# A linear-attention stage with w turned by row halves and its decay scans handed on between half-chunks

## The chip, the cores and the metric

The kernel runs on one core of a Trainium2 chip. Its engines work from queues of their own and meet at semaphores: PE (TensorE), VectorE (DVE in the profile), ScalarE (ACT), GpSimd (POOL), and SP, which here only issues DMAs. Times are device microseconds of one execution; the time before is the median of three runs.

## The reference

Three stages follow each other: a linear attention with decay (B = 4, H = 8, S = 768 tokens, D = 48), a mixture of eight experts of which each token takes the best one, and a dense layer with a squared relu. Only the first stage is touched by the change:

```python
for t in range(S):
    kt, vt, rt, wt = (k[:, :, t], v[:, :, t], r[:, :, t], w[:, :, t])
    cur = np.einsum('bhd,bhe->bhde', u[None] * kt, vt)
    y[:, :, t] = np.einsum('bhd,bhde->bhe', rt, state + cur)
    state = wt[:, :, :, None] * state + np.einsum('bhd,bhe->bhde', kt, vt)
```

## The kernel before, in words

The attention runs over 16 units (`NU`); a unit is one batch row and two heads (`pr`), so that 2 x 64 partitions hold two heads, each padded from 48 to 64. A unit's 768 tokens are `NC` = 6 chunks of `C` = 128. Inputs come in as `nat` tiles with tokens on the partitions.

For one unit the stages are these. `w_turn` (L670) transposes w on PE into two PSUM banks `z`, three chunks in each; a chunk takes `L` = 129 columns, with a zero column between chunks that was set once. `suffix` (L680) scans one bank backwards on VectorE: products of w from a position to the end of its chunk, `suf`. `prefix` (L690) takes the reciprocal of each chunk's whole product as the start (three columns of `f_1`) and scans the same bank forwards, `ff`. Each works on one bank, so a unit has four scans. `k_turn` and `r_turn` (L699, L704) transpose k and r, each into two banks by row halves (twelve 64-row transposes), and VectorE multiplies them with `suf` and `ff` into kT and rA. `scores` (L728) multiplies kT and rA on PE; ScalarE copies the result and GpSimd masks it (L737). `k_back` turns kT back into kP, `states` (L740) multiplies kP with v; for chunk 0 it multiplies with `none`, 64 zero columns of `f_1`. `state_scan` (L747) scans the result on VectorE. `bonus_in`, `within` and `across` add three parts of y in PSUM, `back` transposes y to rows. `gate_products` (L709) are two GpSimd multiplications of 128 x 576 into g1, a tile with one buffer; `gate_sum` (L715) sums it on VectorE, `gate_values` (L719) multiplies v with the sum on GpSimd for bonus_in.

The order on every engine is the order in which the code is written (manual_schedule). The loop `for t in range(-1, NU + 1)` (L838) is a period: it works on unit t and prepares units t + 1 and t + 2. The second half of suffix and prefix of unit t + 1 stands at the head of a period, the first half for unit t + 2 near its end, behind `gate_sum` and `gate_values` of unit t + 1. `step` inserts, by the tables PLAN and LAST, pieces of `route_steps` (L160): the choice of experts for a finished batch row, with many small VectorE operations and scatters by GpSimd. It falls on periods t = 4 to 9, 8 to 13 and 12 to 15.

PSUM banks of the transposes, scores and states come from a ring of four in turn (`Ring`, L642). Within a period the order is scores (2), k_back (2), states (1), scores (2), k_turn (2), r_turn (2), back (2), so the second bank of k_turn is the one that states used.

A load into a `nat` tile is issued by SP at the head of a period, for the unit two periods on (v: one, w: three).

Of the kernel before, what the change touches and what calls it, by code (L numbers as in the profile page):

```python
# [9 lines left out]
F32 = mybir.dt.float32  # L10
# [4 lines left out]
ALU = mybir.AluOpType  # L15
# [6 lines left out]
def rwkv_moe_kernel(  # L22
# [15 lines left out]
    nc = tc.nc  # L38
    B, H, S, D = r.shape
    NT, DM = out.shape  # L40
    E, _, F = w1.shape
    F2 = w_in.shape[1]
    C = 128
    NC = S // C
    HC = NC // 2
    L = C + 1
    HP = H // 2
    KD = DM // 128
    KF = F // 128
# [22 lines left out]
    ident = cst.tile([128, 128], F32, name="ident")  # L72
# [249 lines left out]
    def load_expert(pool, w1e, w2e, hf, into=None):  # L322
        t, t2 = into or (pool.tile([128, KD, F // 2], F32, name="w1r"), pool.tile([128, KF // 2, DM], F32, name="w2r"))
        nc.sync.dma_start(t, w1e.rearrange("o (c p) f -> p (o c) f", p=128)[:, :, hf * (F // 2):(hf + 1) * (F // 2)])
        nc.sync.dma_start(t2, w2e.rearrange("o (c p) d -> p (o c) d", p=128)[:, hf * (KF // 2):(hf + 1) * (KF // 2)])
        return t, t2
# [228 lines left out]
    def first_block(P):  # L555
        return Block(P, NA, w1[0:1], w2[0:1], lambda n, i: gA[:n, 0, i:i + 1])
# [16 lines left out]
    def route_step():  # L573
        return next(routing[B - 1], 0)

    with ExitStack() as actx:
        actx.enter_context(tc.manual_schedule(engines={ET.PE, ET.DVE, ET.Activation, ET.SP, ET.Pool}))
        ac = actx.enter_context(tc.tile_pool(name="ac", bufs=1))
        wk = actx.enter_context(tc.tile_pool(name="wk", bufs=2))
        ps_a = actx.enter_context(tc.tile_pool(name="ps_a", bufs=1, space=PSUM))  # L580
        ps_u = actx.enter_context(tc.tile_pool(name="ps_u", bufs=2, space=PSUM))
        ps_y = actx.enter_context(tc.tile_pool(name="ps_y", bufs=2, space=PSUM))

        NU = B * HP
        HL = HC * L
        NBUF = {"w": 2, "k": 2, "r": 2, "v": 3}
        PAD = {"w": 1.0, "k": 0.0, "r": 0.0, "v": 0.0}
        nat = {(nm, i): ac.tile([128, NC, 2, 64], F32, name=f"{nm}N{i}") for nm in "wkrv" for i in range(NBUF[nm])}
        u_bc = ac.tile([128, H, D], F32, name="u_bc")
        f_1 = ac.tile([128, 1 + NC * L], F32, name="f1")  # L590
        s_1 = ac.tile([128, 1 + HL], F32, name="s1")
        bonus = [ac.tile([128, NC, 2, 64], F32, name=f"gv{i}") for i in range(2)]
        start = [ac.tile([128, 64, NC], F32, name=f"St{i}") for i in range(2)]
        prod = [ac.tile([128, D, NC], F32, name=f"P{i}") for i in range(3)]
        bia = cst.tile([128, 16], F32, name="bia")
        warm = bia[0:1, 2:3]
        none = f_1[:, 2:66]
        zw = [ps_u.tile([128, 1 + HL], F32, name="zw") for _ in range(2)]
        first_z = [ps_y.tile([128, 1 + HL], F32, name="py") for _ in range(2)]
        xTs, xrs = {}, {}  # L600

        def pad(nm, i, eng):
# [9 lines left out]
        def setup_first():  # L612
# [11 lines left out]
            for z in (*zw, *first_z):  # L624
                nc.vector.memset(z[:, ::L], 0.0)
            nc.vector.memset(s_1, 0.0)
            nc.vector.memset(s_1[:, ::L], 1.0)
            nc.vector.memset(f_1, 0.0)
# [23 lines left out]
        class Unit:  # L652
# [15 lines left out]
                return pt  # L668

            def w_turn(self, z=zw):  # L670
                for c in range(NC):
                    hf, ci = divmod(c, HC)
                    nc.tensor.transpose(z[hf][:, 1 + ci * L:1 + ci * L + C], self.wN[:, c].rearrange("p h d -> p (h d)"), ident)

            def w_check(self):
                sq = wk.tile([128, 2 * NC, D], F32, name="sq", bufs=1)
                nc.scalar.activation(sq, self.wN[:, :, :, :D].rearrange("p c h d -> p (c h) d"), AF.Square, bias=bia[:, 0:1])
                nc.scalar.activation(sq, sq, AF.Relu, bias=bia[:, 1:2], accum_out=viol[:, self.un:self.un + 1])

            def suffix(self, hf, z=zw):  # L680
                if hf == 0:
                    self.suf = wk.tile([128, 1 + NC * L], F32, name="suf")
                    self.ff = wk.tile([128, 1 + NC * L], F32, name="ff")
                    self.sufv = self.suf[:, 1:].rearrange("p (c x) -> p c x", x=L)
                    self.fv = self.ff[:, 0:NC * L].rearrange("p (c x) -> p c x", x=L)
                at = hf * HL
                nc.vector.tensor_tensor_scan(out=self.suf[:, at:at + HL + 1][:, ::-1], data0=z[hf][:, ::-1], data1=s_1[:, ::-1],
                                             initial=0.0, op0=ALU.mult, op1=ALU.add)

            def prefix(self, hf, z=zw):  # L690
                at, cs = hf * HL, slice(hf * HC, hf * HC + HC)
                nc.vector.reciprocal(f_1[:, 0:NC * L].rearrange("p (c x) -> p c x", x=L)[:, cs, 0:1], self.sufv[:, cs, 0:1])
                nc.vector.tensor_tensor_scan(out=self.ff[:, at:at + HL], data0=z[hf][:, :HL], data1=f_1[:, at:at + HL],
                                             initial=0.0, op0=ALU.mult, op1=ALU.add)

            def spread(self):
                nc.scalar.copy(self.P[:, :, 1:], self.sufv[:, 1:, 0:1].rearrange("p c o -> p o c").to_broadcast([128, D, NC - 1]))

            def k_turn(self):  # L699
                self.kT = wk.tile([128, NC, C], F32, name="kT")  # L700
                for q, pt in enumerate(self.turn(self.kN.rearrange("p c h d -> p c (h d)"))):
                    nc.vector.tensor_tensor(self.kT[:, :, 64 * q:64 * q + 64], pt, self.sufv[:, :, 1 + 64 * q:65 + 64 * q], op=ALU.mult)

            def r_turn(self):  # L704
                self.rA = wk.tile([128, NC, C], F32, name="rA", bufs=3)
                for q, pt in enumerate(self.turn(self.rN.rearrange("p c h d -> p c (h d)"))):
                    nc.vector.tensor_tensor(self.rA[:, :, 64 * q:64 * q + 64], pt, self.fv[:, :, 64 * q:64 * q + 64], op=ALU.mult)  # L707

            def gate_products(self):  # L709
                eng = nc.vector if self.un == NU - 1 else nc.gpsimd  # L710
# [74 lines left out]
        def at(i, st, *a):  # L785
            if 0 <= i < NU:
                getattr(units[i], st)(*a)
# [21 lines left out]
        def first_block_step(t, place):  # L809

            if t == NU - 3 and place == "loads":
                blkA = first["A"] = first_block(P)
                blkA.upto = NT - S + 1
                words = [load_expert(raw, w1[0:1], w2[0:1], hf) for hf in range(2)]
                blkA.w1r, blkA.w2r = ({hf: words[hf][q] for hf in range(2)} for q in range(2))
            if NU - 2 <= t < NU and place == "back":
                for f in range(2 * (t - NU + 2), 2 * (t - NU + 2) + 2):
                    first["A"].prep_w(f, nc.vector, part="hi")
            if (t, place) == (NU - 1, "back"):
                rows_A(rw)  # L820
            if t == NU - 1 and place == "turned":
                for f in range(FA):
                    first["A"].prep_w(f, nc.vector, part="lo")
            if t == NU - 1 and place == "gate":
                first["A"].gather()
            if t == NU and place == "back":
                first["A"].scale(nc.vector)
            if t == NU and place == "turned":
                routing[B - 1] = route_steps(B - 1, xTs[B - 1], xrs[B - 1], rw, ps_t)
                route_step()  # L830

        setup_first()
        at(0, "w_turn", first_z)
        at(0, "suffix", 0, first_z)
        at(0, "prefix", 0, first_z)
        at(0, "w_check")
        routing_constants()
        for t in range(-1, NU + 1):  # L838
            z = first_z if t == -1 else zw
            load("w", w, t + 3)  # L840
            if t >= 0:
                load("v", v, t + 1)
                load("k", k, t + 2)
                load("r", r, t + 2)
            first_block_step(t, "loads")
            at(t, "scores", 0)
            at(t, "k_back")
            at(t + 2, "w_check")
            step(t, "back")
            first_block_step(t, "back")  # L850
            if t + 1 < NU - 1:
                at(t + 1, "gate_products")
            at(t + 1, "suffix", 1, z)
            at(t + 1, "prefix", 1, z)
            if t == 0:
                at(t, "gate_sum")
                at(t, "gate_values")
            at(t - 1, "within")
            at(t, "states")
            at(t, "state_scan")  # L860
            at(t, "scores", 1)
            at(t + 1, "spread")
            at(t - 1, "across")
            step(t, "scan")
            at(t + 1, "k_turn")
            at(t + 1, "r_turn")
            step(t, "turned")
            first_block_step(t, "turned")
            at(t + 2, "w_turn")
            at(t, "bonus_in")  # L870
            if t + 1 == NU - 1:
                at(t + 1, "gate_products")
            if t >= 0:
                at(t + 1, "gate_sum")
                at(t + 1, "gate_values")
            at(t + 2, "suffix", 0)
            at(t + 2, "prefix", 0)
            step(t, "gate")
            first_block_step(t, "gate")
            if t < NU:  # L880
                at(t - 1, "back")
            step(t, "end")
# [64 lines left out]
    with tc.If(rare > 0, label="rare"):  # L947
        fine = nc.values_load(flag[0:1, 0:1], min_val=0, max_val=1)
        with tc.If(fine == 0):
# [42 lines left out]
            with ExitStack() as fctx:  # L992
# [6 lines left out]
                for b in range(B):  # L999
                    nc.sync.dma_start(xr[:, :, :DM], x_tok[b * S:(b + 1) * S].rearrange("(c p) m -> p c m", p=C))  # L1000
                    for c in range(NC):
                        nc.vector.tensor_copy(xp[:, :, :D], xr[:, c, :DM].rearrange("p (h d) -> p h d", d=D))
                        pt = ps_x.tile([128, 512], F32, name="px")
# [389 lines left out]
```

## Time and profile before

| | |
|---|---|
| median of 3 runs | 838.42 us (837.02 to 838.67) |
| profiled execution | 837.48 us, span 835.6 us |
| PE busy | 805.9 us, 96% |
| VectorE busy | 534.2 us, 64% |
| ScalarE busy | 374.3 us, 45% |
| GpSimd busy | 352.3 us, 42% |
| granted TensorE clock, mean | 0.986 |

The page gives busy time for each engine over the whole span, slices of the span, the chain that ended last and the costliest groups. A timeline lists instructions by start and length (consecutive ones of a kind merged, with their count); in brackets stands how long the engine was idle before and what released it. [...]

### The profile page before, as it was taken

Reading aid. Unit: us, or ns where it says so; the run is one execution under the profiler, and the core shown is the slowest. Engines: PE = TensorE matmul, PEld = TensorE weight load, DVE = VectorE, ACT = ScalarE, POOL = GpSimd, SP = SyncE. Lnnn points to the kernel's source line nnn. Section 1 sums busy time; section 2 is a strip of 40 time slices with the busy share of each in tenths; the row PEclk is TensorE's granted clock in tenths of the full one; section 3 lists DMA queues with packets and bytes.
Section 4 is the critical chain, followed back from the end, with each engine's and each line's share of the span. In section 5 each row is a group of like instructions: output and inputs, shape, how many; then the busy total and the mean of one; then the engine's idle time right before and its main releaser. Section 6 shows DMA issues by size and latency. Waiting matters only on the chain.

```text
span 835.6 us, 15492 instructions
## 1 busy us (share of the span) xinstructions
PE 805.9 (96%) x5868; PEld 731.1 (87%) x5868; DVE 534.2 (64%) x961; ACT 374.3 (45%) x792; POOL 352.3 (42%) x433
## 2 busy tenths in 40 slices
PE   6999999979999999999999999999999999999995
PEld 5988887869889999999999998888899999999994
DVE  7889898946666777887534788888533434434342
ACT  4666665532555455455554343434333333333321
POOL 8666868624434545644752333333211212213121
PEclk9999999969999999999999999999999999999998
DMA  9775769215758676768651232231204213022011
GB/s 181 151 137 115 163 141 271 94 26 179 263 91 214 172 208 219 221 168 248 181 174 33 75 132 76 94 111 62 75 1 142 77 38 114 19 95 76 1 48 38
DMA packets 157365, 102.89 MB, mean 123 GB/s; under 512 B 112351, under 2 KB 140943, under 8 KB 157287
## 3 DMA queue, kind: packets, MB, share of 16 engines
q1 hardware_dynamic: 149046, 86.55, 38.7%
q0 software_dynamic: 4912, 14.65, 5.2%
q8 instruction: 47, 0.77, 0.4%
q10 hardware_dynamic: 3328, 0.66, 0.4%
q14 instruction: 32, 0.25, 0.1%
HBM read 79.34 MB, written 22.50 MB: 122 GB/s over the span
## 4 chain that ended last, share of the span: by engine, by line
PE 59%; issue 12%; POOL 4%; DVE 0%; POOLq 0%; ACT 0%; DVEq 0%; ACTq 0%
PE ph L345 10%; PE ph L344 10%; PE ph L346 10%; PE po L344 5%; PE po L346 5%; PE po L345 5%; PE px L346 5%; PE px L344 5%; PE px L345 5%; POOL out_dram L1182 2%; PE px L430 1%; PE po L430 0%; POOL x22l L339 0%; POOL x21l L339 0%; POOL x20l L339 0%
## 5 line engine op out<-in xcount | busy, mean ns | idle before, releaser
L1157 DVE SCALAR_TENSOR_TENSOR gg<-ph,rl 128x512 f32<-128x512 f32 x96 | 66.2, 690 | 121.6 <-ACT rl L1155 121.6
L1155 ACT ACTIVATE rl<-ph 128x512 f32<-128x512 f32 x96 | 57.4, 598 | 146.4 <-PE ph L346 146.3
L339 DVE TENSOR_TENSOR gl<-gg,gh 128x512 fp32r<-128x512 f32 x96 | 67.0, 697 | 65.9 <-ACT gh L337 41.9
L337 ACT CAST gh<-gg 128x512 fp32r<-128x512 f32 x96 | 59.6, 621 | 103.6 <-DVE gg L1157 103.6
L339 POOL TENSOR_TENSOR w1l<-w1r,w1h 128x384 fp32r<-128x384 f32 x56 | 59.4, 1067 | 66.7 <-ACT w1h L337 66.3
L333 ACT ACTIVATE hh<-ph 128x320 fp32r<-128x320 f32 (+7 forms) x64 | 32.4, 507 | 113.4 <-PE ph L346 107.0
L1103 POOL TENSOR_TENSOR caf<-caf,cbf 128x384 f32<-128x384 f32 x32 | 32.5, 1016 | 114.0 <-DVE cbf L1102 114.0
L339 DVE TENSOR_TENSOR w2l<-w2r,w2h 128x384 fp32r<-128x384 f32 x64 | 64.3, 1007 | 20.1 <-ACT w2h L337 19.5
L334 DVE SCALAR_TENSOR_TENSOR hl<-ph,hh 128x320 fp32r<-128x320 f32 (+7 forms) x64 | 36.9, 576 | 38.3 <-ACT hh L333 38.0
L1182 POOL DMA_INDIRECT out_dram<-ob,tokc x24 | 23.4, 974 | 67.2 <-DVE ob L1180 65.0
L344 PE MATMUL po<-hh,w2h 128*128 128x320 f32 (+4 forms) x120 | 42.8, 357 | 0.0
L345 PE MATMUL po<-hl,w2h 128*128 128x320 f32 (+4 forms) x120 | 41.6, 347 | 0.0
L346 PE MATMUL po<-hh,w2l 128*128 128x320 f32 (+4 forms) x120 | 41.6, 347 | 0.0
L339 POOL TENSOR_TENSOR x22l<-x2r,x22h 128x512 fp32r<-128x512 f32 x12 | 15.5, 1296 | 51.5 <-ACT x22h L337 51.5
L339 POOL TENSOR_TENSOR x21l<-x2r,x21h 128x512 fp32r<-128x512 f32 x12 | 15.5, 1293 | 45.5 <-ACT x21h L337 45.5
L734 PE MATMUL pt<-rA,kT 64*128 64x128 f32 x300 | 31.7, 302 | 2.7 <-DVE rA L707 2.7
L400 POOL DMA_INDIRECT xg<-x_rows,gi x28 | 29.0, 1036 | 11.4 <-issue 5.1
L337 ACT CAST w2h<-w2r 128x384 fp32r<-128x384 f32 x64 | 33.0, 517 | 0.0
L737 POOL TENSOR_SCALAR_AFFINE_SELECT A<-A 128x768 f32<-128x768 f32 x32 | 28.1, 878 | 11.0 <-ACT A L736 10.0
L337 ACT CAST w1h<-w1r 128x384 fp32r<-128x384 f32 x64 | 32.7, 512 | 0.0
L245 POOL DMA_INDIRECT x_rows<-xr,dsi x24 | 24.1, 1003 | 20.3 <-DVE dsi L232 15.3
L339 POOL TENSOR_TENSOR x20l<-x2r,x20h 128x512 fp32r<-128x512 f32 x12 | 15.5, 1291 | 35.9 <-ACT x20h L337 35.9
(859 smaller groups left out, 2661.8 us busy)
## 6 DMA issues: line engine op xcount, KB each, us to landing
w1r<-in_moe_w_dram SPq DMA_DIRECT2D x16, 768.0 KB, 5.5
w2r<-in_moe_w_dram SPq DMA_DIRECT2D x16, 768.0 KB, 7.5
x2r<-x_cols SPq DMA_DIRECT2D x12, 768.0 KB, 4.8
cq<-in_moe_w_in_dram SPq DMA_DIRECT2D x16, 384.0 KB, 5.8
cq<-in_moe_w_out_dram SPq DMA_DIRECT2D x16, 384.0 KB, 8.0
vN<-in_v_dram SPq DMA_DIRECT2D x32, 144.0 KB, 3.9
part<-ob SPq DMA_DIRECT2D x24, 192.0 KB, 2.0
ob<-part SPq DMA_DIRECT2D x24, 192.0 KB, 2.6
```

The source lines that it names most:

```text
L333: nc.scalar.activation(hi, src, AF.Relu)
L334: nc.vector.scalar_tensor_tensor(lo, src, 0.0, hi.bitcast(F32), op0=ALU.max, op1=ALU.subtract)
L337: nc.scalar.copy(hi, src)
L339: lo_eng.tensor_tensor(lo, src, hi.bitcast(F32), op=ALU.subtract)
L344: nc.tensor.matmul(out_, a_of(ah), b_of(bh), start=start, stop=False)
L345: nc.tensor.matmul(out_, a_of(ah), b_of(bl), start=False, stop=False)
L346: nc.tensor.matmul(out_, a_of(al), b_of(bh), start=False, stop=stop)
L734: nc.tensor.matmul(pa[j][:, ci], self.kT[pp, hf * HC + ci], self.rA[pp, hf * HC + ci], start=True, stop=True)
L1103: nc.gpsimd.tensor_tensor(af, af, bf, op=ALU.add)
L1155: nc.scalar.activation(rl, ph, AF.Relu)
L1157: nc.vector.scalar_tensor_tensor(gg, ph, 0.0, rl, op0=ALU.max, op1=ALU.mult)
L1182: ins = nc.gpsimd.indirect_dma_start(out=out[:, :], out_offset=IndirectOffsetOnAxis(ap=tokc[:, n:n + 1], axis=0), in_=ob, in_offset=None)
```

## The change

Each chunk of 128 tokens is cut into two halves of 64 (`HT`). Bank q of `z` now holds half q of all six chunks, 65 columns each (`NL` = 390), and w_turn uses twelve 64-row transposes. The suffix products of the first halves need the product of the second halves: suffix scans bank 1, a copy of six columns puts the products into `f_1`, and bank 0 is scanned with them as starts. In prefix it is the other way round: reciprocal, scan of bank 0, copy of six columns into `f_1`, scan of bank 1. Both scans of suffix for unit t + 2 now stand near the end of the period, both of prefix for unit t + 1 at the head. `suf` and `ff` get an axis for the half, and spread, k_turn and r_turn read them so. gate_products of unit t + 1 moves from behind the first routing pieces to ahead of scores, to the head of the period.

```diff
-    L = C + 1
+    HT = C // 2
+    L = HT + 1
+    NL = NC * L
...
-        f_1 = ac.tile([128, 1 + NC * L], F32, name="f1")
-        s_1 = ac.tile([128, 1 + HL], F32, name="s1")
+        f_1 = ac.tile([128, NL + 1], F32, name="f1")
+        s_1 = ac.tile([128, NL + 1], F32, name="s1")
...
-        none = f_1[:, 2:66]
+        none = f_1[:, 1:L]
...
             def w_turn(self, z=zw):
+
                 for c in range(NC):
-                    hf, ci = divmod(c, HC)
-                    nc.tensor.transpose(z[hf][:, 1 + ci * L:1 + ci * L + C], self.wN[:, c].rearrange("p h d -> p (h d)"), ident)
+                    for q in range(2):
+                        p = slice(HT * q, HT * q + HT)
+                        nc.tensor.transpose(z[q][:, c * L + 1:c * L + L], self.wN[p, c].rearrange("p h d -> p (h d)"), ident[p, p])
...
-                at = hf * HL
-                nc.vector.tensor_tensor_scan(out=self.suf[:, at:at + HL + 1][:, ::-1], data0=z[hf][:, ::-1], data1=s_1[:, ::-1],
-                                             initial=0.0, op0=ALU.mult, op1=ALU.add)
-
-            def prefix(self, hf, z=zw):
-                at, cs = hf * HL, slice(hf * HC, hf * HC + HC)
-                nc.vector.reciprocal(f_1[:, 0:NC * L].rearrange("p (c x) -> p c x", x=L)[:, cs, 0:1], self.sufv[:, cs, 0:1])
-                nc.vector.tensor_tensor_scan(out=self.ff[:, at:at + HL], data0=z[hf][:, :HL], data1=f_1[:, at:at + HL],
-                                             initial=0.0, op0=ALU.mult, op1=ALU.add)
+            def suffix(self, z=zw):
+
+                self.suf = wk.tile([128, 2, NL + 1], F32, name="suf")
+                for q in (1, 0):
+                    if q == 0:
+                        nc.vector.tensor_copy(f_1[:, L::L], self.suf[:, 1, 1::L])
+                    nc.vector.tensor_tensor_scan(out=self.suf[:, q, ::-1], data0=z[q][:, ::-1], data1=(s_1 if q else f_1)[:, ::-1],
+                                                 initial=0.0, op0=ALU.mult, op1=ALU.add)
+
+            def prefix(self, z=zw):
+
+                self.ff = wk.tile([128, 2, NL], F32, name="ff")
+                for q in range(2):
+                    if q == 0:
+                        nc.vector.reciprocal(f_1[:, 0:NL:L], self.suf[:, 0, 1::L])
+                    else:
+                        nc.vector.tensor_copy(f_1[:, 0:NL:L], self.ff[:, 0, HT::L])
+                    nc.vector.tensor_tensor_scan(out=self.ff[:, q], data0=z[q][:, :NL], data1=f_1[:, :NL], initial=0.0, op0=ALU.mult, op1=ALU.add)
...
-        at(0, "suffix", 0, first_z)
-        at(0, "prefix", 0, first_z)
+        at(0, "suffix", first_z)
...
             first_block_step(t, "loads")
+            if t + 1 < NU - 1:
+                at(t + 1, "gate_products")
             at(t, "scores", 0)
...
-            if t + 1 < NU - 1:
-                at(t + 1, "gate_products")
-            at(t + 1, "suffix", 1, z)
-            at(t + 1, "prefix", 1, z)
+            at(t + 1, "prefix", z)
...
-            at(t + 2, "suffix", 0)
-            at(t + 2, "prefix", 0)
+            at(t + 2, "suffix")
```

## Rows read from the trace of the kernel before

**Rows 1.** Busy time by stretch: microseconds and instructions of each engine, granted clock, DMA.

```profile
15.00:165.00 150.00, 143.82 (x2388) 127.45 (x2384) 133.96 (x268) 94.67 (x230) 103.79 (x132) 0.99 0.68 153
```

**Rows 2.** Waits to 180 us: microseconds in total, times, longest.

```profile
DVE kT L702 <- PE pt L667: 6.3, 6, 1.4
```

**Rows 3.** Timeline of VectorE, period t = 3: start, length, operation, idle before.

```profile
37.88 0.74 DVE L717 TENSOR_REDUCE g<-g 128x12 f32<-128x576 f32 x1
38.54 0.96 DVE L687 TENSOR_TENSOR_SCAN suf<-zw,s 128x388 f32<-128x388 f32 x1
39.53 0.18 DVE L692 RECIPROCAL f<-suf 128x3 f32<-128x3 f32 x1
39.74 0.96 DVE L693 TENSOR_TENSOR_SCAN ff<-zw,f 128x387 f32<-128x387 f32 x1
40.62 0.94 DVE L687 TENSOR_TENSOR_SCAN suf<-zw,s 128x388 f32<-128x388 f32 x1
...
42.69 0.73 DVE L749 TENSOR_TENSOR_SCAN St<-pt,P 128x288 f32<-128x288 f32 x1
44.60 0.56 DVE L702 TENSOR_TENSOR kT<-pt,suf 128x384 f32<-128x384 f32 x1 [1.18 <-PE pt L667]
...
46.47 0.74 DVE L717 TENSOR_REDUCE g<-g 128x12 f32<-128x576 f32 x1
```

**Rows 4.** Timeline of GpSimd, the same period.

```profile
38.76 1.15 POOL L720 TENSOR_TENSOR gv<-vN,g 128x576 f32<-128x576 f32 x1 [2.69 <-PE pt L667]
...
40.92 1.42 POOL L712 TENSOR_TENSOR g<-kN,rN 128x576 f32<-128x576 f32 x1
42.42 1.41 POOL L713 TENSOR_TENSOR g<-g,u_bc 128x576 f32<-128x576 f32 x1
```

**Rows 5.** Timeline of PE, the same period and the end of the one before.

```profile
35.82 0.54 PE L667 MATMUL pt<-ident,rN 64*128 64x64 f32 x12
36.29 0.87 PE L673 MATMUL zw<-ident,wN 128*128 128x128 f32 x6
37.00 0.82 PE L758 MATMUL py<-ident,gv 128*128 128x128 f32 x6
...
38.17 0.89 PE L734 MATMUL pt<-rA,kT 64*128 64x128 f32 x12
...
41.78 0.37 PE L734 MATMUL pt<-rA,kT 64*128 64x128 f32 x1
...
43.98 0.59 PE L667 MATMUL pt<-ident,kN 64*128 64x64 f32 x12
```

**Rows 6.** Groups by shape (busy, mean ns), two timeline rows, and one line's shortest, median, longest.

```profile
L258 DVE COPY vA<-vals 128x3 f32<-128x3 f32 x1 | 1.2, 1152 | 0.0
...
L237 DVE COPY vals<-cum 128x8 f32<-128x8 f32 x2 | 0.3, 165 | 0.0
...
101.09 1.46 DVE L190 SCALAR_TENSOR_TENSOR cand<-z,e 128x48 f32<-128x48 f32 x1
...
101.06 1.43 POOL L713 TENSOR_TENSOR g<-g,u_bc 128x576 f32<-128x576 f32 x1
...
L692 DVE RECIPROCAL f<-suf x32: 178/178/181, 6.1 to 151.1; 128x3 f32<-128x3 f32 x32
```

**Rows 7.** Timeline of PE's weight loads, period t = 12: k_turn's second bank.

```profile
130.60 0.14 PEld L667 LDWEIGHTS pt<-ident,kN 64*128 64x128 f32 x1 [0.19 <-DVE St L749]
```

**Rows 8.** Timeline of GpSimd and of PE, period t = 0.

```profile
16.04 1.40 POOL L712 TENSOR_TENSOR g<-kN,rN 128x576 f32<-128x576 f32 x1 [1.33 <-DVE g L717]
...
18.89 1.15 POOL L720 TENSOR_TENSOR gv<-vN,g 128x576 f32<-128x576 f32 x1
...
20.48 0.82 PE L758 MATMUL py<-ident,gv 128*128 128x128 f32 x6
```

**Rows 9.** Timeline of PE and of VectorE, period t = 9.

```profile
101.69 0.27 PE L667 MATMUL pa<-ident,kN 64*128 64x64 f32 x1
...
104.02 0.53 DVE L702 TENSOR_TENSOR kT<-pa,suf 128x384 f32<-128x384 f32 x1
```

More of the change, by code (lines that the diff above doesn't have):

```diff
@@ L584, in rwkv_moe_kernel @@
         NU = B * HP
-        HL = HC * L
         NBUF = {"w": 2, "k": 2, "r": 2, "v": 3}
@@ L596, in rwkv_moe_kernel @@
         warm = bia[0:1, 2:3]
-        none = f_1[:, 2:66]
-        zw = [ps_u.tile([128, 1 + HL], F32, name="zw") for _ in range(2)]
-        first_z = [ps_y.tile([128, 1 + HL], F32, name="py") for _ in range(2)]
+        none = f_1[:, 1:L]
+        zw = [ps_u.tile([128, NL + 1], F32, name="zw") for _ in range(2)]
+        first_z = [ps_y.tile([128, NL + 1], F32, name="py") for _ in range(2)]
         xTs, xrs = {}, {}
@@ L678, in w_check @@
                 nc.scalar.activation(sq, sq, AF.Relu, bias=bia[:, 1:2], accum_out=viol[:, self.un:self.un + 1])
[L680 to L685, printed above, removed]
-                at = hf * HL
-                nc.vector.tensor_tensor_scan(out=self.suf[:, at:at + HL + 1][:, ::-1], data0=z[hf][:, ::-1], data1=s_1[:, ::-1],
-                                             initial=0.0, op0=ALU.mult, op1=ALU.add)
@@ L696, in spread @@
             def spread(self):
-                nc.scalar.copy(self.P[:, :, 1:], self.sufv[:, 1:, 0:1].rearrange("p c o -> p o c").to_broadcast([128, D, NC - 1]))
+                nc.scalar.copy(self.P[:, :, 1:], self.suf[:, 0, L + 1::L].rearrange("p (o c) -> p o c", o=1).to_broadcast([128, D, NC - 1]))
             def k_turn(self):
@@ L701, in k_turn @@
                 for q, pt in enumerate(self.turn(self.kN.rearrange("p c h d -> p c (h d)"))):
-                    nc.vector.tensor_tensor(self.kT[:, :, 64 * q:64 * q + 64], pt, self.sufv[:, :, 1 + 64 * q:65 + 64 * q], op=ALU.mult)
+                    nc.vector.tensor_tensor(self.kT[:, :, 64 * q:64 * q + 64], pt, self.suf[:, q, 1:].rearrange("p (c x) -> p c x", x=L)[:, :, 1:], op=ALU.mult)
             def r_turn(self):
@@ L706, in r_turn @@
                 for q, pt in enumerate(self.turn(self.rN.rearrange("p c h d -> p c (h d)"))):
-                    nc.vector.tensor_tensor(self.rA[:, :, 64 * q:64 * q + 64], pt, self.fv[:, :, 64 * q:64 * q + 64], op=ALU.mult)
+                    nc.vector.tensor_tensor(self.rA[:, :, 64 * q:64 * q + 64], pt, self.ff[:, q].rearrange("p (c x) -> p c x", x=L)[:, :, :HT], op=ALU.mult)
             def gate_products(self):
```

## The prediction

> **What bounds the kernel now.** I read the page's slices first: PE is near full in all of them, so the question is which stage still has another engine in front of PE. The busy times by stretch show it [rows 1]: from 15 to 165 us, the attention stage that the diff edits, VectorE works 134.0 of 150 us, nearly as much as PE. Everything behind 165 us is untouched, so I take the total to move by what this stage moves. Next come the waits [rows 2]: VectorE's product kT waited for PE six times behind a bank pt (a seventh behind pa). In about half of the sixteen periods PE leads; in the others VectorE never waits and leads itself.
>
> Then the timelines of one period without routing work, t = 3, as offsets from the gate_sum that stands at its head, G = 37.88. VectorE [rows 3]: first scan 0.66, reciprocal 1.65, next scan 1.86, second half 2.74, state_scan 4.81 (0.73 long, end 5.54), kT 6.72 after 1.18 us idle, next G 8.59. GpSimd [rows 4]: gate values 0.88 to 2.03, then a mask, gate products from 3.04, 1.50 from the first to the second. PE [rows 5]: states over at 3.90, k_turn at 6.10, so 2.20 between them; kT starts 0.62 after k_turn. One link makes VectorE's order matter to PE: the second bank of k_turn is the one that states filled, and PE may write it only when state_scan has read it. The trace has that wait [rows 7]. So state_scan may slip by 6.10 - 5.54 = 0.56 us before the period grows.
>
> **w_turn.** Six 128-row transposes took 36.29 to 37.00 = 0.71 us of PE [rows 5]; twelve 64-row ones of the form that takes their place took 35.82 to 36.29 = 0.47 (r_turn's). Gain 0.24, bounds 0 and 0.3. But scores of the next unit, started at 38.17, also wait for VectorE's last rA, and gate_sum, queued right behind rA, started at 37.88 [rows 3]: rA was over about then, and with the signal's way to PE 0.1 to 0.2 us are left. Little of the 0.24 can be used: VectorE is late next. I count it only where PE leads by more.
>
> **Scans and copies, nothing in their way.** Before: two chains of scan, reciprocal, scan. A scan followed by what needs it takes 0.99, by anything else 0.88, the small step 0.21 [rows 3]: 4.15 us from 0.66 to 4.81. After: scan, copy, scan, reciprocal, scan, copy, scan = 0.99 + 0.21 + 0.99 + 0.21 + 0.98 + 0.21 + 0.88 = 4.47. Lengths 390 and 391 for 387 and 388 add nothing to speak of. So +0.32, inside the 0.56. The copy's 0.21 is the reciprocal's; a copy of eight elements took 0.165 [rows 6], and 0.1 to 0.3 are the bounds.
>
> **The copies beside GpSimd.** This decides. The copies have their one input and their output in SBUF. The trace has a copy of 3 elements that took 1.152 us while GpSimd multiplied the gate values, and a scalar_tensor_tensor with two SBUF inputs of 1.46 us from 101.09, beside the second gate product's 1.43 from 101.06 [rows 6]: each was held until GpSimd's instruction was over and went on 0.1 later. The reciprocals never were (178 to 181 ns in all 32), nor the scans, which read one operand from PSUM. So the change exchanges half of the reciprocals, which GpSimd doesn't hold, for copies, which it can. [...]
>
> Suffix copy: it stands at 0.66 + 0.99 = 1.65, inside gate values (0.88 to 2.03); what follows starts at 2.13, not 1.86. Then scan, reciprocal, scan put the prefix copy at 2.13 + 0.99 + 0.21 + 0.98 = 4.31. Gate products, moved to the head, follow gate values at once: first 2.05 to 3.46, second 3.55 to 4.96. The copy is held to 4.96, the last scan starts at 5.06, state_scan at 5.94 instead of 4.81: +1.13, of which 0.57 is beyond the cover. Bounds of the two waits: 0 (copies this short may slip in) and 1.4 each (a whole gate product).
>
> [...]
>
> **gate_products at the head, by itself.** Gain: in the periods that choose experts (t = 5, 9, 13) VectorE's small routing steps stand where the gate products were; moved up, these no longer hold them. Cost: GpSimd's queue at t = 0. There the products of unit 1 need the one buffer that gate_sum of unit 0 releases (they waited 1.33 for it [rows 8]), and the mask of scores and the gate values of unit 0 are now queued behind them, and PE's bonus_in behind the gate values. Elsewhere mask and gate values have a period to spare. The loads of k and r are issued a period ahead, so the earlier start finds them there.
>
> **Sum**, period by period:
> - t = -1 to 1: the first prefix ends 0.4 later, the copy for unit 1 meets the gate products of unit 0 (0.5 more), the scans' 0.3 come on top: gate_sum of unit 0 is 1.2 late. Before, products at 16.04, 1.4 each, gate values 18.89 to 20.04, bonus_in free at 20.48 [rows 8]. After: products 17.3 to 20.2, mask 0.87, gate values to 22.2, bonus_in 22.3: +1.8. Bounds 0 and 2.5.
> - t = 2, 3, 4: +0.57 each, +1.7.
> - t = 6, 7, 10, 11: routing steps fill the way from state_scan to kT, so VectorE leads and the 1.13 has no cover. At 6 and 10 the steps end in a copy that a mask holds; a mask holds one of them after as well, and 0.95 passes on. At 7 and 11 two steps of eight elements are held like the 1.46 us one, 0.9 us together, and would be nearly free: +0.33. Together +2.6, bounds 0 and 4.5.
> - t = 8, 12: shorter periods (8.3), worked the same way: +0.55 each, +1.1.
> - t = 5, 9, 13: state_scan waits for PE anyway, by more than 1.1. At 9 k_turn ran at 101.69, so kT could have started at 102.3 but stood at 104.02 behind steps like the 1.46 us one [rows 9]: 1.7, and 0.2 of w_turn, less 0.1 for the mask. The same at 13, 0.5 at 5: -4.1, bounds -5 and -2.
> - t = 14: +0.3, no gate products there on GpSimd.
>
> 1.8 + 1.7 + 2.6 + 1.1 - 4.1 + 0.3 = +3.4 us, in the profiled execution 837.48 + 3.4 = 840.9. The median shown is 838.42; from the middle of the two, 838.0, the forecast is 841.4.
>
> **Rivals.**
> 1. Faster: the copies are not held. Place: the prefix copy at 4.31, the suffix copy at 1.65; it decides from the point where state_scan ends before k_turn comes, 5.13 + 0.73 = 5.86 against 6.10. Then t = 2 to 4 cost nothing, the start 1.2, t = 6, 7, 10, 11 -0.4, t = 8 and 12 +0.4, t = 5, 9, 13 stay at -4.1: -2.9, 835.1 us. For it: a short copy may fall into a gap; against it: the 3-element copy that was held.
> 2. No difference: blocked as forecast, but the stall at t = 0 is absorbed because PE is late there anyway, and t = 5 returns more: 3.4 - 1.8 - 0.4 = +1.2, 839.2. For it: kT waits for PE at t = 0 and at t = 1. Against it: PE stood ready at 20.48, and the gate values come 1.7 us behind that.
> 3. Much slower, and not what the change is meant to do: states reads zeros from f_1 between the columns that the copies write. If the two are ordered as one tile, PE waits for the prefix copy: states from 5.06, k_turn at 5.06 + 0.8 + 2.2 = 8.1, the period 10.5 instead of 8.6, +2 in 14 periods, 866 us. Against it: the pieces don't overlap.
>
> **Chances.** A measurement of this kernel tells about 0.2% (1.7 us) from no change. Forecast 0.57, spread 839 to 844.5 (0.50 slower, 0.07 within); rival 1 0.22 (0.18 faster, 0.04 within); rival 2 0.17 (0.13 within, 0.02 each side); rival 3 0.04, slower. So faster 0.20, within 0.24, slower 0.56. Range 835.0 to 844.0: half of rival 1, rival 3 and the forecast's upper end stay outside. The forecast's own range is 839 to 844.5.
>
> **What would show it.** The copies' durations: many near 0.4 and 0.7 us, rather than 0.165, in periods without routing. state_scan 5.9 after gate_sum, and PE's k_turn released by it. w_turn's twelve in 0.5 us. bonus_in of unit 0 near 22.3, released by gate values. scalar_tensor_tensor of L190 at 0.21 in all three. Wrong: copies all near 0.17 (rival 1), states released by VectorE's copy (rival 3), or a last state_scan less than 1 us later than before (rival 2).

## The result and the profile after

The changed kernel takes 844.30 us (median of 4 runs, 843.21 to 845.32), the kernel before, beside it, 838.14 us (4 runs): ratio 1.0075, interval 1.0058 to 1.0092. It is 6.2 us slower; forecast was 3.4, and 844.30 us lies just above the stated range of 835.0 to 844.0. The profiled execution took 843.21 us with a span of 841.4 us, 5.8 more than before.

First the stretch that the change edits, in the table of busy time by stretch of the changed kernel (length, then busy microseconds and instructions of PE, PEld, DVE, ACT, POOL, the granted clock, the DMA share, GB/s):

```profile
15.00:165.00 150.00, 137.41 (x2391) 120.69 (x2392) 137.81 (x266) 89.92 (x219) 98.79 (x124) 0.99 0.67 149
```

Against [rows 1] PE is busy 6.4 us less in the same 150 us, VectorE 3.9 us more, at the same clock: PE waits more, and VectorE has become longer. The waits of the changed kernel up to 180 us (total, times, longest) say for what:

```profile
PEld pt L668 <- DVE St L755: 5.2, 8, 1.0
...
PE pt L668 <- DVE St L755: 4.0, 7, 0.9
...
DVE kT L708 <- PE pt L668: 2.5, 4, 0.6
```

VectorE's wait for PE at kT has fallen from 6.3 us to 2.5 [rows 2], and in its place k_turn on PE waits for state_scan on VectorE. That is the cover of 0.56 us running out. The same period as in [rows 3], VectorE, in the changed kernel (a start can lie up to 0.09 us ahead of the end of the row above, as at 47.64):

```profile
41.78 0.74 DVE L723 TENSOR_REDUCE g<-g 128x12 f32<-128x576 f32 x1
42.44 0.96 DVE L689 TENSOR_TENSOR_SCAN suf<-zw,s 128x391 f32<-128x391 f32 x1
43.43 0.41 DVE L688 COPY f<-suf 128x6 f32<-128x6 f32 x1
43.88 0.97 DVE L689 TENSOR_TENSOR_SCAN suf<-zw,f 128x391 f32<-128x391 f32 x1
44.88 0.19 DVE L697 RECIPROCAL f<-suf 128x6 f32<-128x6 f32 x1
45.11 0.97 DVE L700 TENSOR_TENSOR_SCAN ff<-zw,f 128x390 f32<-128x390 f32 x1
46.11 0.61 DVE L699 COPY f<-ff 128x6 f32<-128x6 f32 x1
46.76 0.97 DVE L700 TENSOR_TENSOR_SCAN ff<-zw,f 128x390 f32<-128x390 f32 x1
47.64 0.73 DVE L755 TENSOR_TENSOR_SCAN St<-pt,P 128x288 f32<-128x288 f32 x1
49.00 1.02 DVE L708 TENSOR_TENSOR kT<-pt,suf 128x384 f32<-128x384 f32 x2 [0.63 <-PE pt L668]
...
50.87 0.74 DVE L723 TENSOR_REDUCE g<-g 128x12 f32<-128x576 f32 x1
```

GpSimd in the same period of the changed kernel, and PE:

```profile
42.66 1.15 POOL L726 TENSOR_TENSOR gv<-vN,g 128x576 f32<-128x576 f32 x1 [3.41 <-PE pt L668]
43.77 1.43 POOL L718 TENSOR_TENSOR g<-kN,rN 128x576 f32<-128x576 f32 x1
45.27 1.42 POOL L719 TENSOR_TENSOR g<-g,u_bc 128x576 f32<-128x576 f32 x1
```

```profile
40.08 0.59 PE L676 MATMUL zw<-ident,wN 64*128 64x64 f32 x12
40.60 0.88 PE L764 MATMUL py<-ident,gv 128*128 128x128 f32 x6
...
48.43 0.52 PE L668 MATMUL pt<-ident,kN 64*128 64x64 f32 x10 [0.51 <-DVE St L755]
```

The suffix copy, issued at 43.43 inside the gate values (42.66 to 43.81), is over at 43.84. The prefix copy, issued at 46.11 inside the second gate product (to 46.69), is over at 46.72. So each is held to the end of the GpSimd instruction beside it, as forecast. state_scan starts 5.86 us after gate_sum, k_turn follows its end (48.37), and the period is 9.09 us instead of 8.59.

That is as forecast; two places are not. The first is t = 9, on VectorE and on GpSimd:

```profile
99.25 0.74 DVE L723 TENSOR_REDUCE g<-g 128x12 f32<-128x576 f32 x1
99.91 0.96 DVE L689 TENSOR_TENSOR_SCAN suf<-zw,s 128x391 f32<-128x391 f32 x1
100.90 2.40 DVE L688 COPY f<-suf 128x6 f32<-128x6 f32 x1
103.33 0.97 DVE L689 TENSOR_TENSOR_SCAN suf<-zw,f 128x391 f32<-128x391 f32 x1
```

```profile
99.69 0.98 POOL L247 DMA_INDIRECT x_rows<-xr,dsi  x1 [0.18 <-issue]
100.70 1.17 POOL L726 TENSOR_TENSOR gv<-vN,g 128x576 f32<-128x576 f32 x1
101.79 0.09 POOL L811 MEMSET bia<- 1x1 f32 x1
101.84 1.42 POOL L718 TENSOR_TENSOR g<-kN,rN 128x576 f32<-128x576 f32 x1
```

Here a routing piece put a scatter (DMA_INDIRECT) ahead of the gate values. The copy, issued 0.20 us into them, did not go on when they ended at 101.87, but only after the first gate product, at 103.30. The same happens at t = 13 (141.80, 2.39 us). The groups of line 688, line 699 and line 192 (shortest, median, longest in ns; first and last start) show how rare that is:

```profile
L688 DVE COPY f<-suf x16: 248/408/2397, 6.0 to 154.0; 128x6 f32<-128x6 f32 x16
```

```profile
L699 DVE COPY f<-ff x16: 172/496/637, 8.6 to 158.0; 128x6 f32<-128x6 f32 x16
```

```profile
L192 DVE SCALAR_TENSOR_TENSOR cand<-z,e x4: 208/208/211, 67.2 to 184.2; 128x48 f32<-128x48 f32 x4
```

The last one was the good half of the forecast: the step of 1.46 us [rows 6] takes 0.21 everywhere.

The second place is the start. GpSimd, then PE, in the changed kernel:

```profile
17.31 1.42 POOL L718 TENSOR_TENSOR g<-kN,rN 128x576 f32<-128x576 f32 x1 [4.21 <-DVE g L723]
18.80 1.42 POOL L719 TENSOR_TENSOR g<-g,u_bc 128x576 f32<-128x576 f32 x1
20.18 0.88 POOL L743 TENSOR_SCALAR_AFFINE_SELECT A<-A 128x768 f32<-128x768 f32 x1
21.05 1.14 POOL L726 TENSOR_TENSOR gv<-vN,g 128x576 f32<-128x576 f32 x1
```

```profile
22.24 0.87 PE L764 MATMUL py<-ident,gv 128*128 128x128 f32 x6 [1.87 <-POOL gv L726]
...
24.66 2.72 PE L771 MATMUL py<-A,vN 128*64 128x128 f32 x24
...
43.30 1.53 PE L771 MATMUL py<-A,vN 128*64 128x128 f32 x24
```

The queue is the one forecast, and bonus_in starts at 22.24 (forecast 22.3; 20.48 before [rows 8]). But the 24 matmuls of `within` that follow took 2.72 us instead of the 1.53 of a later period. The stretches of the changed kernel show PE's granted clock there (columns as above):

```profile
23.00:24.00 1.00, 1.00 (x18) 0.96 (x17) 0.96 (x2) 0.00 (x0) 1.00 (x2) 0.87 1.10 210
24.00:25.00 1.00, 1.00 (x18) 0.88 (x16) 0.93 (x3) 0.88 (x3) 1.00 (x2) 0.50 1.14 226
...
26.00:27.00 1.00, 1.00 (x12) 1.00 (x12) 0.54 (x1) 0.97 (x2) 1.00 (x2) 0.50 1.05 211
```

Some 1.5 us after the idle 1.87 us PE's granted clock fell from 1.00 to 0.50 and stayed there for some 3 us. In the kernel before the granted clock is 1.00 from 20 to 32 us.

The sixteen starts of gate_sum cut the stage as the forecast did. Each figure is the change of the intervals between them, in us; the last column is one of the experiments below.

| term | forecast | measured | with both losses taken out |
|---|---|---|---|
| start, to the gate_sum at the head of t = 2 | +1.8 | +3.39 | +1.08 |
| t = 2, 3, 4 | +1.7 | +1.50 | +1.45 |
| t = 5, 9, 13 | -4.1 | -0.75 | -3.04 |
| t = 6, 7, 10, 11 | +2.6 | +1.47 | +1.66 |
| t = 8, 12 | +1.1 | +1.12 | +1.12 |
| t = 14 | +0.3 | +0.11 | +0.10 |
| last gate_sum to the end of the span | 0 | -1.04 | +0.53 |
| span | +3.4 | +5.8 | +2.9 |

The figures come from one profiled execution of each kernel. Two rows depend on which execution was profiled: the start came out at +3.22, +3.29 and +4.73 in three later kernels with the same order at t = 0, and the way from the last gate_sum to the end, which no edit touches, lay between -1.90 and +0.90 in the twelve traces beside the one before. Up to the last gate_sum the change is 6.84 us late.

### The profile page after: what moved, and what is told of

It reads as the page before. It is cut to its first block, busy times and chain, and to the rows that moved or that the text cites. A ratio compares the mean times of both kernels' runs of the same rounds, so it can differ in the third digit from the quotient of the medians.

```text
span 841.4 us, 15700 instructions
## 1 busy us (share of the span) xinstructions
PE 801.0 (95%) x5964; PEld 725.0 (86%) x5964; DVE 543.2 (65%) x977; ACT 374.1 (44%) x792; POOL 351.9 (42%) x433
## 4 chain that ended last, share of the span: by engine, by line
PE 62%; DVE 15%; issue 14%; POOL 4%; DMA 2%; ACT 0%; POOLq 0%; DVEq 0%; SPq 0%; ACTq 0%
PE ph L346 9%; PE ph L347 9%; PE ph L348 9%; PE po L346 5%; PE po L348 5%; PE px L348 5%; PE po L347 5%; PE px L346 5%; PE px L347 5%; DVE suf L689 3%; POOL out_dram L1185 2%; DVE ff L700 2%; DVE rA L713 2%; DVE kT L708 1%; DVE St L755 1%
## 5 line engine op out<-in xcount | busy, mean ns | idle before, releaser
L726 POOL TENSOR_TENSOR gv<-vN,g 128x576 f32<-128x576 f32 x16 | 18.4, 1153 | 32.1 <-issue 14.2
```

## The experiments

Two theories stood at first. One: both edits of the change act as forecast, one of them mis-sized. The other: they hurt each other, the copies being held by the products that were moved next to them. So each was run alone.

**The scans alone** (gate products where they were):

```diff
-            if t + 1 < NU - 1:
-                at(t + 1, "gate_products")
             at(t, "scores", 0)
...
+            if t + 1 < NU - 1:
+                at(t + 1, "gate_products")
             at(t + 1, "prefix", z)
```

> The change's scans, copies and w_turn, with gate_products left where they stood before. Theory A (copies held by GpSimd, and the queue at t = 0): the prefix copy at 4.3 after gate_sum now meets the end of the first gate product instead of the second, so plain periods grow by about 0.2 rather than 0.5; no stall of bonus_in at t = 0; the routing steps stay held as before: +2 to +3 us against before. Theory C (moving gate_products is what costs, the scans are neutral): no difference from before, within 0.7 us.

844.34 us, ratio 1.0074 (1.0057 to 1.0092): as slow as the whole change, a size that no theory had. A plain period takes 8.65 us, only 0.06 more than before: the suffix copy is still held (0.41), the prefix copy is free (0.17), and one held copy fits under the cover. The loss lies elsewhere: the start is 2.63 us late (PE idle 1.04 us, then slow matmuls), t = 6 costs 0.6, and t = 10 took 11.89 us, 2.79 more than before, with slow matmuls: the 24 of `within` from 112.78 took 2.83 us, those from 101.23 took 1.53. They were seen in the one profiled execution; whether the other five had them isn't shown. At t = 9 the copy behind the scatter took 1.21 us, to the end of the gate values; no gate product stood behind them:

```profile
98.86 1.21 DVE L688 COPY f<-suf 128x6 f32<-128x6 f32 x1
```

```profile
97.81 1.01 POOL L247 DMA_INDIRECT x_rows<-xr,dsi  x1 [0.15 <-issue]
98.86 1.16 POOL L726 TENSOR_TENSOR gv<-vN,g 128x576 f32<-128x576 f32 x1
```

**The move alone** (the kernel before with the gate products at the head):

```diff
             first_block_step(t, "loads")
+            if t + 1 < NU - 1:
+                at(t + 1, "gate_products")
             at(t, "scores", 0)
...
-            if t + 1 < NU - 1:
-                at(t + 1, "gate_products")
             at(t + 1, "suffix", 1, z)
```

> Only gate_products at the head of the period; w_turn, scans and reciprocals as before, no copies. Theory A: at t = 0 bonus_in waits about 0.5 to 1 us for gate values; afterwards the routing steps at t = 7, 9, 11, 13 are no longer held by gate products (0.9, 1.7, 0.9, 1.7 us), nothing is added: -3 to -5 us. Theory C: slower than before by 3 us or more.

835.96 us, ratio 0.9980 (0.9969 to 0.9992): 2.2 us faster where 3 to 5 were expected. t = 9 took 11.49 us for 12.33, t = 13 11.59 for 12.25, t = 5 11.21 for 11.45, so -1.74 together; t = 7, 8, 11 and 12 return another 0.96, and the start costs 0.53. So the move by itself is a gain of 2.2 us, and the scans by themselves a loss of 6.2; together they lose 6.2, not 4.0. Here the second theory holds: the two halves hurt each other. Added to the scans, the move returns 1.07 at t = 5, 9 and 13 (-0.75 in the change, +0.32 with the scans alone), but costs 1.33 at t = 2, 3 and 4 (+1.50 and +0.17), where it puts the second product beside the prefix copy.

**The copies as an operation that GpSimd doesn't hold.** The two copies become a maximum over an axis of length one, on the same engine:

```diff
-                        nc.vector.tensor_copy(f_1[:, L::L], self.suf[:, 1, 1::L])
+                        nc.vector.tensor_reduce(f_1[:, L::L], self.suf[:, 1, 1::L].rearrange("p (c o) -> p c o", o=1), axis=AX.X, op=ALU.max)
...
-                        nc.vector.tensor_copy(f_1[:, 0:NL:L], self.ff[:, 0, HT::L])
+                        nc.vector.tensor_reduce(f_1[:, 0:NL:L], self.ff[:, 0, HT::L].rearrange("p (c o) -> p c o", o=1), axis=AX.X, op=ALU.max)
```

> The change with the two copies written as a sum-free reduction over an axis of length one (tensor_reduce, max) on the same engine, same values, which reads one operand and, like gate_sum, was never held by GpSimd. Theory A: each takes about 0.16 to 0.2 us everywhere, the 2.4 us ones are gone, plain periods are back to 8.6 us; the stall at t = 0 stays (2 to 3 us): total from -2.5 to +0.5 us against before. Theory B (the longer chain of scans by itself costs, whatever its copies wait): still +4 us or more.

836.60 us, ratio 0.9980 (0.9970 to 0.9990), from 1.0075 by these two lines alone; -1.5 us against before lies inside the -2.5 to +0.5 expected. The groups of the two lines in this kernel:

```profile
L688 DVE TENSOR_REDUCE f<-suf x16: 164/166/169, 6.1 to 148.3; 128x6 f32<-128x6 f32 x16
```

```profile
L699 DVE TENSOR_REDUCE f<-ff x16: 165/166/167, 8.5 to 152.4; 128x6 f32<-128x6 f32 x16
```

None of the 32 was held, beside the same GpSimd instructions that held the copies. A plain period takes 8.40 us (before 8.59), t = 9 and t = 13 11.21. So holding is the cause of what the plain periods lost, and the new scans by themselves make it 0.19 us shorter. The start remained: t = 1 took 12.62 us, after PE had waited 1.36 us for the gate values.

**The order at t = 0.** First the products of unit 1 at their old place in that one period:

```diff
-            if t + 1 < NU - 1:
+            if t != 0 and t + 1 < NU - 1:
                 at(t + 1, "gate_products")
...
             first_block_step(t, "back")
+            if t == 0:
+                at(t + 1, "gate_products")
```

> The change, but at t = 0 alone gate_products stay behind scores and k_back, as before. Theory A: bonus_in at t = 0 no longer waits 1.9 us, PE's clock does not fall behind it, gate_sum of t = 1 comes 2 to 3 us earlier than in the change: +3 to +4 us against before instead of +6. If the slow start has another cause: unchanged, +6.

842.91 us, ratio 1.0057 (1.0041 to 1.0073): +4.8 us, not the +3 to +4 expected. PE still waits 1.04 us, and the gate_sum of t = 2 is still 2.5 us late: at the old place, too, the gate values of unit 0 stand behind the products. They have to stand ahead of them. So the same edit (with the condition t != 0 at the head of the period), one step further down, was put on three kernels:

```diff
...
             if t == 0:
                 at(t, "gate_sum")
                 at(t, "gate_values")
+                at(t + 1, "gate_products")
```

On the change with the copies:

> The change with its copies, and at t = 0 alone gate_products of unit 1 behind gate values of unit 0. Theory A: gate_sum of t = 1 near 29.8 instead of 32.7, the rest as in the change: +3 to +4 us against before instead of +6. Otherwise: +6.

841.83 us, ratio 1.0053 (1.0038 to 1.0068), +4.7 us where +3 to +4 was expected; bonus_in of unit 0 starts at 20.37, no wait in front of it, and the gate_sum of t = 2 comes at 30.39 instead of 32.69. On the change with the reductions:

> The change with reductions in place of the copies, and at t = 0 alone gate_products of unit 1 behind gate values of unit 0 on GpSimd. Theory A (the queue at t = 0 lets PE idle, and its clock falls behind it): bonus_in of unit 0 starts as soon as w_turn is over, near 20.4, PE's clock stays at its upper level from 20 to 28 us, gate_sum of t = 1 near 29.5 instead of 33.2: 3 to 4 us less than with the reductions alone, -4 to -6 us against before. If the slow start comes from elsewhere: as with the reductions alone, -1.5.

834.15 us, ratio 0.9966 (0.9955 to 0.9976); bonus_in starts at 19.70, gate_sum of t = 2 at 29.27. That is 3.9 us earlier than with the reductions alone, as expected, but the total is only 3.0 us under before and not 4 to 6. In the profiled executions the end behind the last gate_sum takes 2.8 us of the gain back (-1.90 with the reductions alone, +0.90 here). On the kernel before with the move alone:

> The kernel before with gate_products at the head of the period, except that at t = 0 they stand behind gate values of unit 0; scans as before. Theory A: the move alone lost 0.7 us in the first periods, which comes back: -2.5 to -3.5 us against before. Otherwise: -2, as the move alone.

833.00 us, ratio 0.9959 (0.9943 to 0.9974), gate_sum of t = 2 at 28.50. This is the fastest kernel of the case, 4.1 us under the one before, without any of the new scans; its interval and that of the one with reductions overlap.

**What makes the copy lose its turn at t = 9 and 13.** Suspected first was the small memset between the gate values and the gate products, which a plain period doesn't have. It was left out ahead of a block's first routing piece:

```diff
-                        apart()
+                        if (t - HP * b, place) != plan[0]:
+                            apart()
```

> The change without the one-element memset that GpSimd runs ahead of the first routing piece (it stood between gate values and the gate products in the periods that end at t = 4, 8, 12). Theory M (the memset between them costs the waiting copy its turn): the two copies of 2.4 us fall to about 1.0, gate_sum of t = 9 and of t = 13 come 1 to 1.4 us earlier, +3.5 us against before. Theory S (what counts is the scatter that GpSimd runs ahead of gate values there, and the memset is harmless): the two copies stay at 2.4 us, +6.

844.40 us, ratio 1.0083 (1.0064 to 1.0102). The copies still took 2.37 and 2.35 us: the theory of the memset falls. Next the scatter was moved from the end of t = 8 and 12 to the middle of t = 9 and 13, in the table of routing pieces:

```diff
-                (7, "turned"), (7, "gate"), (8, "back"), (8, "turned"), (9, "back"), (9, "turned"))
+                (7, "turned"), (7, "gate"), (8, "back"), (9, "back"), (9, "scan"), (9, "turned"))
```

> The change, with the scatter of the token ids moved from the turned step of t = 8 and 12 to the scan step of t = 9 and 13, so that at the end of t = 8 and 12 no scatter stands ahead of the gate values on GpSimd. Theory S (the copy loses its turn because the gate values come late, behind the scatter): the two suffix copies of 2.39 and 2.40 us fall to about 0.4 us, the intervals from t = 8 to 10 and from t = 12 to 14 shorten by 1.3 to 1.8 us each, and the kernel comes to about 3.5 us over the kernel before (ratio near 1.004). Rival T (the copy loses its turn for another reason, as the candidates' steps or the semaphores of those periods): copies of 2.4 us stay, ratio stays near 1.0075. Rival U: the copies shorten but the scatter in the scan step holds the gate products or another copy instead by about its own 0.98 us: ratio 1.006 to 1.008.

842.38 us, ratio 1.0043 (1.0028 to 1.0058): copy and ratio are what the theory of the scatter gave, but the two periods shortened by 1.10 us each and not by 1.3 to 1.8. VectorE and GpSimd of this kernel at t = 9:

```profile
100.72 0.41 DVE L688 COPY f<-suf 128x6 f32<-128x6 f32 x1
...
103.39 0.65 DVE L699 COPY f<-ff 128x6 f32<-128x6 f32 x1
```

```profile
99.94 1.15 POOL L726 TENSOR_TENSOR gv<-vN,g 128x576 f32<-128x576 f32 x1 [0.64 <-issue]
...
101.08 1.42 POOL L718 TENSOR_TENSOR g<-kN,rN 128x576 f32<-128x576 f32 x1
```

The copy is 1.99 us shorter, of which the prefix copy, now meeting the second product, takes back 0.48; the period falls from 12.16 us to 11.06. But the scatter had done two things: it stood there, and it made the gate values late, so that the copy was issued 0.20 us into them instead of 0.8. In the last pair the lateness was made without a scatter, by three small copies on GpSimd at the end of t = 2 and 3:

```diff
+        late_g = ac.tile([128, NC, 2], F32, name="late_g")
...
+                if t in (2, 3):
+                    for _ in range(3):
+                        nc.gpsimd.tensor_copy(late_g, units[t + 1].g)
                 at(t + 1, "gate_values")
```

> The change, with three GpSimd copies of 12 elements (of g, into a scratch tile) ahead of the gate values at t = 2 and 3 alone, where no scatter runs, so that the gate values begin about 1.4 us after the gate sum and the suffix copy is issued some 0.2 us into them, as at t = 9. If the lateness of the gate values is to blame, the suffix copy takes about 2.4 us in those two periods, through gate values and first gate product; if the scatter itself is to blame, it takes about 1.0 us, to the end of the gate values alone. All other periods stay as in the change.

One execution, 846.02 us. VectorE and GpSimd of this kernel at t = 3:

```profile
43.32 1.00 DVE L688 COPY f<-suf 128x6 f32<-128x6 f32 x1
```

```profile
42.47 0.70 POOL L882 COPY late_g<-g 128x12 f32<-128x12 f32 x3 [3.33 <-DVE g L723]
43.14 1.16 POOL L726 TENSOR_TENSOR gv<-vN,g 128x576 f32<-128x576 f32 x1
44.25 1.42 POOL L718 TENSOR_TENSOR g<-kN,rN 128x576 f32<-128x576 f32 x1
```

The copy was issued 0.18 us into gate values that followed the copies without a gap, with a gate product waiting behind, and still got its turn when they ended, after 1.00 us; the same at t = 4, while at t = 9 and 13 of the same execution it took 2.39 and 2.40. So early issue alone is not it. A scatter alone is not it either. At t = 10 of the kernel with the moved scatter one ended 0.08 us ahead of the gate values, and a gate product stood behind them:

```profile
111.78 0.41 DVE L688 COPY f<-suf 128x6 f32<-128x6 f32 x1
```

```profile
109.95 0.97 POOL L247 DMA_INDIRECT x_rows<-xr,dsi  x1 [0.16 <-DVE rA L713]
111.00 1.15 POOL L726 TENSOR_TENSOR gv<-vN,g 128x576 f32<-128x576 f32 x1
112.11 1.42 POOL L718 TENSOR_TENSOR g<-kN,rN 128x576 f32<-128x576 f32 x1
```

This copy, issued 0.78 us into the gate values, went on when they ended; the kernel of the next pair of edits, below, gives 0.41 at the same place too. In all ten places where a copy lost its turn (t = 9 and 13 of five kernels) a scatter just ahead and an issue 0.20 to 0.22 us into the gate values come together. Neither was enough by itself. Whether the two together are the cause, and how a scatter has an effect one instruction later, isn't shown by any run.

**Both losses out.** The order at t = 0 and the moved scatter together, the copies kept:

> The change with two edits at once: at t = 0 the gate products behind the gate values of unit 0, and the scatter of the token ids out of t = 8 and 12. Theory: the start and the two lost copies are separate losses, worth 2.5 us (843.4 to 840.9 of difference to before, as measured alone) and 1.9 us, so together they take 4.2 to 4.6 us off the change: the difference to the kernel before falls from 6.2 to 1.6 to 2.0 us, ratio 1.0015 to 1.003, with the suffix copy of unit 0 to 15 never over 0.8 us. Rival: the start's gain is spent elsewhere once the two copies are short (PE or the weights' stage sets the end): difference 3 to 4 us, ratio over 1.0035.

840.27 us against 838.59, ratio 1.0022 (1.0010 to 1.0033), longest suffix copy 0.60 us. The two losses are separate and add up: about 4.5 of the 6.2 us are gone. What is left is in the last column of the table above, from its profiled execution of 840.33 us; that one differs from the profiled execution before by 2.9 us, the medians by 1.7.

Turning w by halves with the old scans was not tried.

## Why the prediction was right in direction and too small

- **Copies held by GpSimd**: right, and it decides. Copies of 0.41 and 0.61 us, state_scan 5.86 us after gate_sum, k_turn released by it, +0.50 a period for the 0.57 forecast. A copy that nothing holds took 0.17 us (line 699), near the row of 0.165. The reductions, which aren't held, turn the sign. Rival 1 and rival 3 fall.
- **t = 5, 9, 13, -4.1: the step that failed.** It measured -0.75 (-0.47, -0.17, -0.11). The routing steps did become short, and the move alone returned 1.74. But the term took the copy's price of a plain period for these too, and let state_scan wait for PE in any case. At t = 9 and 13 the trace of before has a scatter as the last routing piece of the period in front of the gate values. Behind it, issued 0.20 us into the gate values, the suffix copy took 2.40 us instead of 0.41, and state_scan started at 106.67 with no wait for PE. With the scatter elsewhere the term is -3.04, inside the bounds -5 and -2 given for it. Looking at GpSimd's queue just ahead of the gate values in each kind of period, not only at t = 3, would have shown a different neighbour; that it costs a second instruction could not be read from any row.
- **The start, +1.8**: the place and the time of bonus_in were right to 0.1 us, the price wasn't: +3.39. PE's idle 1.87 us was followed by matmuls at a granted clock of 0.50, 2.72 us instead of 1.53 for `within`. This is the second term that was mis-sized: the forecast priced the wait and not what PE does after it. With no wait there (both losses taken out) the start costs 1.08. Rival 2 (absorbed) falls.
- **t = 6, 7, 10, 11, +2.6**: +1.47; t = 7 and 11, forecast at +0.33 each, cost 0.08 and 0.06, t = 6 and 10 0.66 and 0.67 for 0.95. **t = 8, 12**: +1.12 for 1.1. **t = 14**: nearly nothing, as said.
- **w_turn**: twelve transposes from 40.08 to 40.60, 0.52 us; right, and not to be seen in the period's length while state_scan sets it.
- **The end, 0**: -1.04. From the last gate_sum to the end the profiled execution of the change is shorter, in part because before the granted clock was at 0.50 from 174 to 187 us, after only from 181 to 187. It isn't the change's doing by any experiment here: in the slices of six kernels (the one before and the change among them) the granted clock is 0.6 to 0.8 around 167 to 188 us, and the kernel with both losses out has +0.53 there.

So two terms were mis-sized by 3.4 and 1.6 us to the bad side, and the smaller misses and the end, some 2.5 us, to the good side. The 1.0 us of the end is luck. Without it the stage is 6.84 us late, twice the forecast.

## What to carry to other kernels

A copy of six elements between two scans took 0.17 us here where nothing held it and up to 2.40 us where GpSimd's work beside it did, so look up the other engine's work at that moment in every kind of period, routing and scatters included, and where it can't be avoided use an operation that isn't held: here two lines took the ratio from 1.0075 to 0.9980, 7.7 us. Test the two halves of a change apart; the half that was slow carried one that gained 2.2 us, and 4.1 with one more line. A wait that is put in front of TensorE need not be priced at its own length, here 1.87 us of idle time in a start that costs 3.39: look at the duration of the matmuls behind it.

## What the runs showed of the hardware

- A VectorE copy of 6 elements, issued 0.20 to 0.22 us into a GpSimd multiplication that followed a scatter, was held through this and the next GpSimd multiplication, 2.35 to 2.40 us, in all ten places with a gate product behind. Without a scatter (0.41, 1.00 us) or issued 0.78 us into it behind a scatter (0.41 us) it went on at the end of the first.
- A reduction over an axis of length one does the same copy in 164 to 169 ns and was held in none of 32 places.
- After an idle stretch of PE at 20 to 22 us, matmuls took up to 1.8 times as long for some us. In the changed kernel (1.87 us idle) the granted clock shows it, 0.50 for some 3 us. In four others, with 1.04 (twice), 1.36 and 1.84 us idle, the six matmuls of bonus_in took 1.54 us instead of 0.87 while the rows give a clock of 1.00. There PE had been as slow ahead of the wait already (w_turn 0.94 to 0.96 us, 0.59 at t = 3). With the same slow w_turn and no wait, in the change with the gate products behind, bonus_in took 1.10 and `within` its usual 1.53. In the move alone, with 1.17 us idle, the matmuls took their usual time ahead of the wait and behind it (0.87). In the five kernels without a wait there, the one before among them, `within` never took longer than 1.53 us. So the length of the wait doesn't decide by itself; what does is open.
